# All twelve pairs of the last two tiles projected by seven products, with the order of their output products changed

## The chip, the cores and the metric

The kernel runs on one core of a Trainium2 chip. The metric is the device time of one execution in microseconds (us); the time before is the median of three runs. The trace is that of one profiled execution.

## The reference, cut to what matters

```python
scores = (q @ k^T) / sqrt(64)               # batch 8, heads 8, sequence 576, head size 64
masks  = local (0 <= i-j < 32) for heads 0-3, strided (i-j >= 0, i = j mod 32) for heads 4-7
attn   = softmax(where(mask, scores, -1e9)) @ v
x      = attn.transpose(0, 2, 1, 3).reshape(4608, 512)
a, b   = x @ w_a, x @ w_b                   # w_a, w_b: 512 x 1536
out    = (a * b) @ w_out                    # w_out: 1536 x 512
```

Inputs and output are float32; the kernel multiplies in bfloat16 and sums in float32.

## The kernel before, in words

**Tiles and slots.** The 4608 rows of x are worked off in nine tiles `t` of 512 tokens (`NT` = 9). A tile has 16 slots, and slot `16*t + s` is the unit in which everything is placed. In slots 0 to 11 the first projection is made for one block `f` of 128 of the 1536 inner columns: `a = x w_a`, `b = x w_b`, then VectorE writes `pf = a*b`. In slots 12 to 15 the output projection of the tile is made. A batch of attention has 576 tokens, so batch 7, the last, gives the last 64 tokens of tile 7 and all of tile 8. The attention steps of batch b (`S`: scores and exponential, `V`: product with v and normalisation into `xT`) are interleaved with the slots of the tiles before by a table: `LATER` by slot, `IN_Y` by the number of output products that are done. Heads are taken in eight units; `V4` to `V7` are the strided ones, whose results go straight into the fourth and third 128-row chunk of `xT` (`step_VT`: product on TensorE, a logarithm and an exponential on ScalarE, L534 and L535, two multiplications on VectorE, L541).

**Seven products.** Two places use the seven-product form of a 2x2 block product (Strassen's, in Winograd's variant).
- The output projection of tiles 2 to 8 (`FAST_Y`). Six blocks g of the inner sum, each of 128, are summed for every product k = "1" to "7" and each half q of the tokens: 14 (k, q) times 6 matmuls of 256 columns. Left operands are blocks of `pf` or sums of them, `ps`, which `fast_s(t, n, blocks)` makes on VectorE (n = 0 to 3). Sum n = 2, the operand of product 7, needs only the even half (e = 0) of each pair's `pf`. The products go to three PSUM banks X, Y, Z, and in X and Z one product is added upon another: product 6 accumulates on product 1 in X, so X must have been read out by the copy after 1 (`y_post`, ScalarE, L785) before the first matmul of 6 may write. Tiles 2 to 7 use `y_plan` (both halves q in one bank), tile 8 uses `y_tail` (one bank for each half, stored half by half).
- The first projection of some pairs g (blocks f = 2g and 2g + 1) of tiles 7 and 8 (`FAST_A`, `a_pair`): only `a` is made this way, by seven products of two matmuls of 256 columns, `b` plainly by eight matmuls of 512 columns. Its sums are `wsum_make` of w_a (in slots of tile 6) and `xsum_make(t, n)` of x.

**One pair.** `a_pair` issues on TensorE: product 1, three matmuls of b(1), product 6, one of b(1), products 7 and 2, product 5, two of b(0), products 4 and 3, two of b(0). Each product's bank is evacuated by ScalarE or added by VectorE as soon as it is there. X is read out after 1 before 6 is added. At the end `mult(1)` and then `mult(0)` form `pf` for the two blocks (L711). Its banks are given by hand: for odd g, `got[1]`, the bank of b(1), is the single buffer `tp`, and the rest are the three rotating buffers `mm`; for even g `tp` holds product 2.

**Banks.** After the start PSUM is three buffers `mm`, one `tp`, two banks `st` and two banks `o`. Plain blocks and the output projection take theirs by `mm_bank`, which counts its calls from slot 16 on and gives `tp` to every fourth:

```python
def mm_bank(shape):
    nm = "tp" if used[0] % 4 == 3 and used[0] >= 0 else "mm"
    used[0] += 1
...
        bank = {x: mm_bank([128, 2, HN]) for x in "ZXY"}     # y_plan
...
        banks = [{x: mm_bank([128, HN]) for x in "ZXY"},     # y_tail
```

A plain block takes two, a tile's output stage three (tile 1, which isn't in `FAST_Y`, four; the second halves of `y_tail` use `o`, `st` and two more). A buffer that is taken again waits until the last reader of its old content is done.

**Order.** The order on each engine is that of the program. `do(slot, ...)` and `soon` put sums behind a slot, `take` runs the attention steps.

Of the kernel before, what the change touches and what calls it, by code (L numbers as in the profile page):

```python
# [24 lines left out]
VW = 128  # L25
WCH = (0, 2, 5, 9, 12)
FAST_Y = (2, 3, 4, 5, 6, 7, 8)
FAST_A = {7: (1, 2, 3, 4), 8: (0, 1, 2, 3)}


@with_exitstack
def kernel(
# [531 lines left out]
    def step_X(b, c):  # L564
# [21 lines left out]
             10: "S6",  # L586
             11: "V5"}
    IN_Y = {2: "S7", 6: "V6", 11: "V7"}
    FN = {"Tk": step_Tk, "Tq": step_Tq, "S": step_S, "V": step_V, "X": step_X, "W": lambda b, n: fast_w(n, slice(0, 3)),
          "s": S_px, "m": S_m, "L": lead_vl, "O": rows_out, "I": rows_in, "Pk": lambda b, c: pair_up("k", c), "Pq": lambda b, c: pair_up("q", c),  # L590
          "Z": lambda b, n: zero_qz(0, nc.vector, ((1, 1),)), "D": lambda b, n: step_D(FIRST_D, 0, "k", n)}

    def run(b, slot):
# [83 lines left out]
    def a_pair(t, g):  # L677

        pf = pfs[t]
        pool, nm = ((pst, "st"), (psum4["o"], "o"))[g % 2]  # L680
        X = pool.tile([128, 2, 512], F32, tag=nm, name="ax")[:, 0, :HT]
        a = ([fsb.tile([128, TTOK], F32, tag="a_sb", name="a_sb") for _ in range(2)] if g % 2 == 0 else
             [t.rearrange("p h n -> p (h n)")[:, :2 * TTOK].bitcast(F32) for t in kT_buf[0]])
        got = {k: psum4[nm].tile([128, TTOK], F32, tag=nm, name="mm")
               for k, nm in zip((1, "Z", "Y", 0), (("mm", "mm", "tp", "mm"), ("tp", "mm", "mm", "mm"))[g % 2])}
        Z, Y = got["Z"][:, :HT], got["Y"][:, :HT]
        p7 = fsb.tile([128, HT], F32, tag="p7", name="p7")
        quarter = lambda e, k: a[e][:, HT * k:HT * (k + 1)]
        w = lambda e, j: (lambda c: wav[:, j, c, g, e])
        ws = lambda n: (lambda c: wsum_a[n][:, c, g])  # L690
        x = lambda j, k: (lambda c: x_part(t, j, k)[:, c])
        xs = lambda n: (lambda c: xsum[t][:, n, c])
        plan = {"1": (X, w(0, 0), x(0, 0)), "2": (Y, w(0, 1), x(1, 0)), "3": (X, ws(3), x(1, 1)), "4": (Z, w(1, 1), xs(3)),
                "5": (X, ws(0), xs(0)), "6": (X, ws(1), xs(1)), "7": (Z, ws(2), xs(2))}

        def P(k):
            bank, lhs, rhs = plan[k]
            for c in range(2):
                nc.tensor.matmul(bank, lhsT=lhs(c), rhs=rhs(c), start=k in "172" and c == 0, stop=c == 1, skip_group_check=True)  # L699

        x0 = TTOK * t % (XR * S)

        def b_mm(e, kks):
            f = 2 * g + e
            for kk in kks:
                nc.tensor.matmul(got[e], lhsT=wb_sb[:, kk, 128 * f:128 * (f + 1)], rhs=xT[:, kk, x0:x0 + TTOK],  # L706
                                 start=kk == 0, stop=kk == KD - 1)

        def mult(e):
            halves = lambda v_: v_.rearrange("p (a i s) -> p a i s", i=2, s=16)  # L710
            nc.vector.tensor_mul(pf[:, 2 * g + e, :].rearrange("p (i a s) -> p a i s", i=2, s=16),  # L711
                                 halves(a[e]), halves(got[e]))

        P("1")
        nc.scalar.copy(quarter(0, 0), X)
        b_mm(1, (0, 1, 2))
        P("6")
        nc.scalar.copy(quarter(1, 0), X)
        b_mm(1, (3,))
        P("7")  # L720
        nc.scalar.copy(p7, Z)
        P("2")
        nc.vector.tensor_tensor(quarter(0, 0), Y, quarter(0, 0), op=ALU.add)
        yield None
        P("5")
        nc.scalar.copy(quarter(1, 1), X)
        nc.gpsimd.tensor_tensor(quarter(1, 1), quarter(1, 1), p7, op=ALU.add)
        if (t, g - 1) in later:
            later.pop((t, g - 1))()
        b_mm(0, (0, 1))  # L730
        P("4")
        nc.vector.tensor_tensor(quarter(1, 0), Z, quarter(1, 0), op=ALU.add)
        P("3")
        nc.scalar.copy(quarter(0, 1), X)
        b_mm(0, (2, 3))
        mult(1)
        mult(0)
        yield pf[:1, 2 * g + 1, :1]

    later = {}  # L740
# [3 lines left out]
    def fast_s(t, n, gs):  # L744
        if t not in pss:
            pss[t] = nat.tile([128, FG * 5 * SW], BF16, tag="shared", name="ps").rearrange("p (n g m) -> p n g m", g=FG, n=5)
        s = pss[t][:, :, gs, :HT]
        x = pfs[t].rearrange("p (g e) (i m) -> p e i g m", e=2, i=2)[:, :, :, gs]
        a, b, op = ((x[:, 0, 1], x[:, 1, 1], ALU.add), (s[:, 0], x[:, 0, 0], ALU.subtract),
                    (x[:, 0, 0], x[:, 0, 1], ALU.subtract), (x[:, 1, 0], s[:, 1], ALU.subtract))[n]  # L750
        if (t, n) == (NT - 1, 2) and {gs.start, gs.start + 1} <= set(FAST_A[t]):
            later[t, gs.start] = lambda: nc.gpsimd.tensor_tensor(s[:, n], a, b, op=op)
            return
        nc.vector.tensor_tensor(s[:, n], a, b, op=op)
# [36 lines left out]
            nc.scalar.copy(part(0, 1), bank)  # L791

    Y_ORDER = [(x[0], int(x[1])) for x in "10 11 70 71 60 61 40 41 50 51 20 21 30 31".split()]
    TAIL_ORDER = [(x[0], int(x[1])) for x in "10 70 60 11 40 50 71 30 61 20 51 41 31 21".split()]

    def y_plan(t):

        plan, y = products(t), y_bufs()
        bank = {x: mm_bank([128, 2, HN]) for x in "ZXY"}

        def store_half(i):
            rows = out[TTOK * t:TTOK * (t + 1)].rearrange("(a i s q) c -> a s i (q c)", i=2, s=8, q=2)
            nc.sync.dma_start(out=rows[:, :, i], in_=y[i].rearrange("p q c -> p (q c)"))

        for n, (k, q) in enumerate(Y_ORDER):
            b, lhs, rhs = plan[k]
            for g in range(FG):
                nc.tensor.matmul(bank[b][:, q], lhsT=lhs(g, q), rhs=rhs(g), start=k in "172" and q == 0 and g == 0,  # L808
                                 stop=g == FG - 1, skip_group_check=True)
                if g == FG - 1:  # L810
                    if q == 1:
                        y_post(k, y, slice(0, 2), bank[b])
                        if k == "5":
                            y_post("+", y, slice(0, 2), None)
                    take(("y", t, n + 1))
                yield y
        do(16 * t + 18, store_half, 0)
        do(16 * t + 19, store_half, 1)

    def y_tail(t):  # L820
# [2 lines left out]
        banks = [{x: mm_bank([128, HN]) for x in "ZXY"},  # L823
                 {"X": psum4["o"].tile([128, 2, 512], F32, tag="o", name="end")[:, 0, :HN],
                  "Z": pst.tile([128, 2, 512], F32, tag="st", name="end")[:, 0, :HN]}]
        for k, q in TAIL_ORDER:
            b, lhs, rhs = plan[k]
            cuts = [slice(0, HN)]
            if (q, k) == (1, "2"):
                cuts = [slice(0, 128), slice(128, HN)]  # L830
            for n in cuts:
                if (q, k) == (1, "2"):
                    bank = mm_bank([128, 128])
                else:
                    bank = banks[q][b]
                for g in range(FG):
                    nc.tensor.matmul(bank, lhsT=lhs(g, q), rhs=rhs(g)[:, n], start=g == 0 and k in "172",  # L837
                                     stop=g == FG - 1, skip_group_check=True)
                    if g < FG - 1:
                        yield y  # L840
                y_post(k, y, q, bank, n)
                if k == "5":
                    y_post("+", y, q, None)
# [10 lines left out]
    def ffn_ys(t, j, mid):  # L854
        if j == 0:
            yst[t] = (y_tail if t == NT - 1 else y_plan)(t)
        for i in range(21):
            y = next(yst[t])
            if i == 10:
                mid()  # L860
        if j == 3:
            for _ in yst[t]:
                pass
        return (y[0][:1, 0, :1], None, y[1][:1, 0, HN:HN + 1], y[1][:1, 0, :1])[j]

    def ffn_y(t, j, mid):
        pf = pfs[t]
# [33 lines left out]
    with tc.manual_schedule(engines={ENG.PE, ENG.SP, ENG.Pool, ENG.DVE, ENG.Activation}):  # L901
# [76 lines left out]
        for b in range(1, B):  # L978
            for pos, names in (STEPS.get(b) or {16 * (b - 1) + x: n for x, n in LATER.items()}).items():
                steps.setdefault(pos, []).append((b, names.split()))  # L980
            if b not in STEPS:
                for n, names in IN_Y.items():
                    steps["y", b - 1, n] = [(b, names.split())]
        steps[16 * (B - 2) + 9][-1][1].append("I1")

# [4 lines left out]

        soon = {}
        for t in FAST_Y[:-1]:
            soon[16 * t + 10] = [lambda t=t: fast_s(t, 2, slice(4, 6))]
            soon[16 * t + 11] = [lambda t=t, n=n: fast_s(t, n, slice(4, 6)) for n in (0, 1)]
        do(0, fill_v, vl_buf[0])
        do(0, fill_v, vs_buf[0])
        for c in range(4):
# [21 lines left out]
                    do(g0 + g, step_D, b, z, nm, part)  # L1019
        for n in range(4):  # L1020
            do(16 * (NT - 3) + 2 * n + 2, wsum_make, n)
        do(16 * (NT - 2) - 1, xsum_make, NT - 2, 0)
        for n in (2, 1, 3):
            do(16 * (NT - 2), xsum_make, NT - 2, n)
        for n in range(4):
            do(16 * (NT - 2) + 12 + n, xsum_make, NT - 1, n)
        for h in range(HL):
            do((7, 7, 8, 9)[h], spread_vs, 1, h, nc.vector.tensor_copy)
        do(1, zero_qz, 1, nc.vector, ((1, 1),))
# [57 lines left out]
```

## Time and profile before

| | |
|---|---|
| median of 3 runs | 326.13 us (326.02 to 326.52) |
| profiled execution, its own time | 326.3 us |
| span of its trace | 324.6 us |
| granted TensorE clock, mean | 0.998 |
| TensorE (PE) busy | 317.0 us, 98% of the span |
| VectorE (DVE) busy | 258.5 us, 80% |
| ScalarE (ACT) busy | 188.9 us, 58% |
| GpSimd (POOL) busy | 160.3 us, 49% |

The profiled execution's own time is 1.7 us more than its span. In the rows, PE is TensorE's matmuls and PEld its weight loads; a row of the timeline gives the start, the duration, engine, line, operation, what is written from what, how many instructions of a kind are merged in the row, and in brackets the engine's idle time ahead of it and what ended that. A matmul's row is longer than the distance to the next one, since matmuls are pipelined; what a stage costs is read from the starts.

### The profile page before, as it was taken

Reading aid. Unit: us, or ns where it says so; the run is one execution under the profiler, and the core shown is the slowest. Engines: PE = TensorE matmul, PEld = TensorE weight load, DVE = VectorE, ACT = ScalarE, POOL = GpSimd, SP = SyncE. Lnnn points to the kernel's source line nnn. Section 1 sums busy time; section 2 is a strip of 40 time slices with the busy share of each in tenths; the row PEclk is TensorE's granted clock in tenths of the full one; section 3 lists DMA queues with packets and bytes.
Section 4 is the critical chain, followed back from the end, with each engine's and each line's share of the span. In section 5 each row is a group of like instructions: output and inputs, shape, how many; then the busy total and the mean of one; then the engine's idle time right before and its main releaser. Section 6 shows DMA issues by size and latency. Waiting matters only on the chain.

```text
span 324.6 us, 7425 instructions
## 1 busy us (share of the span) xinstructions
PE 317.0 (98%) x2651; PEld 209.4 (65%) x2680; DVE 258.5 (80%) x559; ACT 188.9 (58%) x329; POOL 160.3 (49%) x289
## 2 busy tenths in 40 slices
PE   8999999999999999999999999999999999999994
PEld 7754555455555587557999885569455966686573
DVE  6767888888778899898889888988999768837842
ACT  6763775478764576447644764476546655335441
POOL 8945837699857554853576247644013012203300
PEclk9999999999999999999999999999999999999999
DMA  9999999899999999999999979999145040004004
GB/s 154 154 204 201 203 185 174 170 181 132 139 213 136 133 95 98 118 218 131 107 107 191 172 90 108 174 174 120 43 108 140 14 129 3 0 0 131 0 3 129
DMA packets 110724, 40.43 MB, mean 125 GB/s; under 512 B 88672, under 2 KB 107744, under 8 KB 110688
## 3 DMA queue, kind: packets, MB, share of 16 engines
q0 software_dynamic: 85968, 19.48, 65.1%
q1 hardware_dynamic: 24576, 20.42, 25.3%
q8 instruction: 21, 0.34, 0.5%
q14 instruction: 15, 0.12, 0.1%
q10 hardware_dynamic: 144, 0.07, 0.1%
HBM read 39.51 MB, written 10.91 MB: 155 GB/s over the span
## 4 chain that ended last, share of the span: by engine, by line
PE 88%; DMA 6%; POOL 2%; ACT 1%; DVE 1%; issue 1%; POOLq 0%
PE mm L622 46%; PE mm L808 14%; PE mm L872 6%; PE st L388 4%; PE mm L706 4%; PE o L466 2%; PE ax L699 2%; DMA xd<-xl 2%; PE o L525 2%; DMA xT<-xd 2%; DMA vl<-in_v_dram 2%; PE mm L699 2%; PE mm L837 2%; POOL shared L197 1%; PE end L837 1%; PE ab L622 1%
## 5 line engine op out<-in xcount | busy, mean ns | idle before, releaser
L622 PE MATMUL mm<-xT,wb_sb 128*128 128x512 bf16 (+1 forms) x404 | 93.3, 354 | 0.4
L622 PE MATMUL mm<-xT,wa_sb 128*128 128x512 bf16 (+1 forms) x391 | 92.1, 353 | 1.0 <-DMA xT<-xd 0.2
L643 ACT COPY a_sb<-mm 128x512 f32<-128x512 f32 x90 | 52.7, 586 | 53.8 <-PE mm L622 51.8
L622 PEld LDWEIGHTS <-wb_sb 128*128 128x128 bf16 x416 | 40.2, 98 | 36.6 <-DVE pf L711 0.4
L1053 POOL CAST pace<-pf 1x1 f32<-1x1 bf16 x83 | 24.9, 300 | 71.2 <-DVE pf L646 51.6
L646 DVE TENSOR_TENSOR pf<-a_sb,mm 128x512 bf16<-128x512 f32 x68 | 46.2, 680 | 9.6 <-PE mm L622 8.1
L622 PEld LDWEIGHTS <-wa_sb 128*128 128x128 bf16 x416 | 37.5, 98 | 24.4 <-issue 0.5
L409 ACT ACTIVATE p<-st 72x576 bf16<-72x576 f32 (+1 forms) x56 | 36.4, 650 | 14.4 <-PE st L388 14.2
L541 DVE TENSOR_TENSOR xT<-o,xr 64x288 bf16<-64x288 f32 x48 | 21.4, 446 | 14.8 <-ACT xr L535 14.3
L808 PEld LDWEIGHTS <-ps 128*128 128x128 bf16 x288 | 28.0, 98 | 3.1
L785 ACT COPY y_sb<-mm 128x512 f32<-128x512 f32 (+1 forms) x28 | 15.6, 556 | 17.9 <-PE mm L808 15.3
L808 PE MATMUL mm<-wf,ps 128*128 128x256 bf16 x216 | 25.5, 273 | 0.0
L534 ACT ACTIVATE xr<-o 64x576 f32<-64x576 f32 x28 | 18.1, 648 | 11.9 <-PE o L525 11.6
L872 PE MATMUL mm<-wo_sb,pf 128*128 128x512 bf16 x93 | 23.0, 379 | 0.2
L243 POOL DMA_DIRECT2D vs<-in_v_dram x24 | 19.6, 820 | 4.9 <-PE mm L808 2.4
L808 PEld LDWEIGHTS <-pf 128*128 128x128 bf16 x216 | 20.3, 98 | 2.6 <-issue 0.2
L1053 POOL COPY pace<-y_sb 1x1 f32<-1x1 f32 x23 | 5.2, 226 | 33.1 <-DVE y_sb L783 19.8
L535 ACT ACTIVATE xr<-xr 64x576 f32<-64x576 f32 x28 | 19.1, 683 | 0.9
L212 POOL DMA_DIRECT2D ql<-in_q_dram x24 | 16.0, 666 | 5.8 <-DMA wo_sb<-in_moe_w_out_dram 4.9
L808 PE MATMUL mm<-wo_sb,pf 128*128 128x256 bf16 x144 | 18.5, 273 | 0.1
L212 POOL DMA_DIRECT2D kl<-in_k_dram x24 | 16.1, 670 | 4.7 <-issue 3.9
L706 PE MATMUL mm<-xT,wb_sb 128*128 128x512 bf16 x60 | 18.3, 379 | 0.1
(189 smaller groups left out, 566.6 us busy)
## 6 DMA issues: line engine op xcount, KB each, us to landing
out_dram<-y_sb SPq DMA_DIRECT2D x12, 512.0 KB, 6.0
out_dram<-y_sb SPq DMA_DIRECT2D x11, 256.0 KB, 4.0
vl<-in_v_dram POOLq DMA_DIRECT2D x6, 384.0 KB, 8.2
kl<-in_k_dram POOLq DMA_DIRECT2D x24, 72.0 KB, 3.2
ql<-in_q_dram POOLq DMA_DIRECT2D x24, 72.0 KB, 3.4
vs<-in_v_dram POOLq DMA_DIRECT2D x24, 72.0 KB, 4.3
wo_sb<-in_moe_w_out_dram POOLq DMA_DIRECT2D x4, 384.0 KB, 9.7
natk<-in_k_dram POOLq DMA_DIRECT2D x20, 72.0 KB, 3.6
```

The lines of the kernel that those rows point to most:

```text
L212: nc.gpsimd.dma_start(out=t[32 * h:32 * h + 32], in_=src[b, h].rearrange("(i y) d -> y i d", y=32))
L243: nc.gpsimd.dma_start(out=vs_buf[b % 2][:, h, :, 0:D], in_=v[b, HL + h].rearrange("(p r) d -> p r d", r=RS))
L409: nc.scalar.activation(p_flat(p)[:M, :2 * W].rearrange("p (i n) -> p i n", n=2 * n), st[:M].rearrange("p a (i n) -> p (a i) n", n=256)[:, ...
L535: nc.scalar.activation(r, r, ACT.Exp, scale=-1.0)
L541: nc.vector.tensor_mul(dst.rearrange("d (p r) -> d p r", r=RS)[:, :, G * half:G * (half + 1)], o[:64, j, :W].rearrange("d (g p) -> d p g", ...
L622: nc.tensor.matmul(ps_[:, c0:c0 + n], lhsT=w[:, kk, 128 * f:128 * (f + 1)], rhs=xT[:, kk, x0:x0 + n], start=(kk == first and c0 == 0), sto ...
L643: nc.scalar.copy(a_sb, ab[0])
L646: nc.vector.tensor_mul(pf[:, f, :].rearrange("p (i a s) -> p a i s", i=2, s=16), halves(a_sb), halves(ab[1]))
L706: nc.tensor.matmul(got[e], lhsT=wb_sb[:, kk, 128 * f:128 * (f + 1)], rhs=xT[:, kk, x0:x0 + TTOK], start=kk == 0, stop=kk == KD - 1)
L808: nc.tensor.matmul(bank[b][:, q], lhsT=lhs(g, q), rhs=rhs(g), start=k in "172" and q == 0 and g == 0, stop=g == FG - 1, skip_group_check=True)
L872: nc.tensor.matmul(ybank[j], lhsT=pf[:, f, 128 * j:128 * (j + 1)], rhs=wo_sb[:, f], start=(f == 0), stop=(f == FD - 1))
L1053: nc.gpsimd.tensor_copy(pace, done)
```

## The change

- `FAST_A` takes all six pairs of tiles 7 and 8: pairs 0 and 5 of tile 7 and pairs 4 and 5 of tile 8 go from two plain blocks each to `a_pair`.
- In pair 5 `mult(0)` comes ahead of `mult(1)`.
- The order of the output products: a lead of some products has its first five blocks done for all of them, and then their last blocks. In tile 7 the lead is 10 11 70 71, in tile 8 it is 10 70 11, where 11 is also moved ahead of 60.
- Batch 7's `V6` runs after the fifth output product of tile 6 and not the sixth, `V7` after the ninth and not the eleventh; the sums of x for tile 7 (`T0` to `T3`) follow them there, and are no longer behind slots 111 and 112.
- In tile 7 the sum n = 2 of blocks 4 and 5 follows slot 11 and not slot 10; the sums of x for tile 8 follow slots 125 and 126 and not 124 to 127; one sum of each pair of tile 8 but the last goes to GpSimd.

```diff
-FAST_A = {7: (1, 2, 3, 4), 8: (0, 1, 2, 3)}
+FAST_A = {7: range(6), 8: range(6)}
...
     IN_Y = {2: "S7", 6: "V6", 11: "V7"}
+    IN_Y_LAST = {2: "S7", 5: "V6 T0", 9: "V7 T1 T2 T3"}
...
+          "T": lambda b, n: xsum_make(NT - 2, n), ...
...
-        mult(1)
-        mult(0)
+        for e in (0, 1) if g == FG - 1 else (1, 0):
+            mult(e)
...
-        if (t, n) == (NT - 1, 2) and {gs.start, gs.start + 1} <= set(FAST_A[t]):
+        if (t, n) == (NT - 1, 2) and gs.start + 1 in FAST_A[t]:
             later[t, gs.start] = lambda: nc.gpsimd.tensor_tensor(s[:, n], a, b, op=op)
...
     Y_ORDER = [(x[0], int(x[1])) for x in "10 11 70 71 60 61 40 41 50 51 20 21 30 31".split()]
-    TAIL_ORDER = [(x[0], int(x[1])) for x in "10 70 60 11 40 50 71 30 61 20 51 41 31 21".split()]
+    TAIL_ORDER = [(x[0], int(x[1])) for x in "10 70 11 60 40 50 71 30 61 20 51 41 31 21".split()]
+
+    def blockwise(order, lead):
+
+        head = order[:lead]
+        return [(k, q, g) for k, q in head for g in range(FG - 1)] + [(k, q, FG - 1) for k, q in head] + [
+            (k, q, g) for k, q in order[lead:] for g in range(FG)]
...
-        for n, (k, q) in enumerate(Y_ORDER):
+        for k, q, g in blockwise(Y_ORDER, 4 if t in FAST_A else 0):
...
-        for k, q in TAIL_ORDER:
+        for k, q, g in blockwise(TAIL_ORDER, 3):
...
-                for n, names in IN_Y.items():
+                for n, names in (IN_Y_LAST if b == B - 1 else IN_Y).items():
...
         for t in FAST_Y[:-1]:
-            soon[16 * t + 10] = [lambda t=t: fast_s(t, 2, slice(4, 6))]
-            soon[16 * t + 11] = [lambda t=t, n=n: fast_s(t, n, slice(4, 6)) for n in (0, 1)]
+            for n in (2, 0, 1):
+                soon.setdefault(16 * t + (10 if n == 2 and t not in FAST_A else 11), []).append(
+                    lambda t=t, n=n: fast_s(t, n, slice(4, 6)))
...
-        do(16 * (NT - 2) - 1, xsum_make, NT - 2, 0)
-        for n in (2, 1, 3):
-            do(16 * (NT - 2), xsum_make, NT - 2, n)
         for n in range(4):
-            do(16 * (NT - 2) + 12 + n, xsum_make, NT - 1, n)
+            do(16 * (NT - 2) + 13 + n // 2, xsum_make, NT - 1, n)
```

More of the change, by code (lines that the diff above doesn't have):

```diff
@@ L588 @@
     IN_Y = {2: "S7", 6: "V6", 11: "V7"}
+    IN_Y_LAST = {2: "S7", 5: "V6 T0", 9: "V7 T1 T2 T3"}
     FN = {"Tk": step_Tk, "Tq": step_Tq, "S": step_S, "V": step_V, "X": step_X, "W": lambda b, n: fast_w(n, slice(0, 3)),
-          "s": S_px, "m": S_m, "L": lead_vl, "O": rows_out, "I": rows_in, "Pk": lambda b, c: pair_up("k", c), "Pq": lambda b, c: pair_up("q", c),
+          "T": lambda b, n: xsum_make(NT - 2, n), "s": S_px, "m": S_m, "L": lead_vl, "O": rows_out, "I": rows_in, "Pk": lambda b, c: pair_up("k", c), "Pq": lambda b, c: pair_up("q", c),
           "Z": lambda b, n: zero_qz(0, nc.vector, ((1, 1),)), "D": lambda b, n: step_D(FIRST_D, 0, "k", n)}
@@ L803, in store_half @@
             nc.sync.dma_start(out=rows[:, :, i], in_=y[i].rearrange("p q c -> p (q c)"))
-        for n, (k, q) in enumerate(Y_ORDER):
+        for k, q, g in blockwise(Y_ORDER, 4 if t in FAST_A else 0):
             b, lhs, rhs = plan[k]
[L807 to L816, printed above, removed]
+            nc.tensor.matmul(bank[b][:, q], lhsT=lhs(g, q), rhs=rhs(g), start=k in "172" and q == 0 and g == 0,
+                             stop=g == FG - 1, skip_group_check=True)
+            if g == FG - 1:
+                if q == 1:
+                    y_post(k, y, slice(0, 2), bank[b])
+                    if k == "5":
+                        y_post("+", y, slice(0, 2), None)
+                take(("y", t, Y_ORDER.index((k, q)) + 1))
+            yield y
         do(16 * t + 18, store_half, 0)
@@ L829, in y_tail @@
             if (q, k) == (1, "2"):
+                if g:
+                    continue
                 cuts = [slice(0, 128), slice(128, HN)]
             for n in cuts:
+                bank, gs = banks[q].get(b), (g,)
                 if (q, k) == (1, "2"):
[L833 to L836, printed above, removed]
+                    bank, gs = mm_bank([128, 128]), range(FG)
+                for g in gs:
                     nc.tensor.matmul(bank, lhsT=lhs(g, q), rhs=rhs(g)[:, n], start=g == 0 and k in "172",
@@ L840, in y_tail @@
                         yield y
+                if g < FG - 1:
+                    continue
                 y_post(k, y, q, bank, n)
@@ L863, in ffn_ys @@
                 pass
-        return (y[0][:1, 0, :1], None, y[1][:1, 0, HN:HN + 1], y[1][:1, 0, :1])[j]
+        return (None if t in FAST_A else y[0][:1, 0, :1], None, y[1][:1, 0, HN:HN + 1], y[1][:1, 0, :1])[j]
     def ffn_y(t, j, mid):
```

## The prediction

> **What bounds the kernel now.** I read the page first. The chain that ended last is TensorE's own work:
>
> ```profile
> PE 88%; DMA 6%; POOL 2%; ACT 1%; DVE 1%; issue 1%; POOLq 0%
> ```
>
> Then I cut the trace at the starts of the changed stages (columns: length, busy us and count for PE, PEld, DVE, ACT, POOL, then granted clock, DMA share, GB/s):
>
> ```profile
> 261.33:264.78 3.45, 3.40 (x17) 1.57 (x16) 2.67 (x7) 1.76 (x3) 0.24 (x1) 1.00 0.29 58
> 264.78:277.80 13.02, 12.92 (x87) 8.60 (x88) 10.13 (x22) 7.31 (x20) 3.37 (x7) 1.00 0.19 67
> 277.80:281.26 3.46, 3.46 (x17) 1.57 (x17) 3.10 (x7) 1.32 (x3) 0.64 (x3) 1.00 0.00 0
> 290.43:293.92 3.49, 3.35 (x23) 2.15 (x22) 0.96 (x3) 2.21 (x6) 0.65 (x1) 1.00 0.42 87
> 303.69:310.64 6.95, 6.90 (x33) 3.06 (x33) 5.34 (x14) 2.54 (x5) 1.19 (x4) 1.00 0.00 1
> ```
>
> These are tile 7's plain pair 0, its four seven-product pairs, its plain pair 5; tile 8's seven-product pair 0, and its two plain pairs 4 and 5. PE hardly pauses, and the output stages (281.26 to 290.43 and 310.64 to 319.84) are 9.17 and 9.20 us for 84 matmuls' worth each, 0.109 us a matmul, with no gap. So a matmul saved is time saved, and any wait put in front of PE is time lost.
>
> **What is removed.** Four plain pairs cost 3.45 + 3.46 + 6.95 = 13.86 us. The four pairs between 264.78 and 277.80 cost 13.02, 3.255 each. Four conversions give -0.84 us; that is the ceiling of the gain. The extra work on the other engines (seven evacuations a pair, GpSimd's sum) is in those 13.02 us already and hidden there.
>
> A rule speaks against this part. The Trainium skill, "TensorE: Matmul & The Clock Gate", section "Back-to-back issue gap", gives 131 ns for a sustained 512-column matmul and 81 ns for 128 columns; put between them, 256 columns would be about 98 ns (my estimate), so 14 small matmuls would cost more than the 8 large ones they replace, 1.37 against 1.05 us, and four conversions +1.3 us instead of a gain. The rows of this trace disagree with it: 512 columns follow at 0.2155 us here and 256 at 0.109, and the four pairs' 13.02 us are measured. By the rule the sum below would end at 331.3 us; it gets no chance of its own.
>
> **Tile 7, pair 0: +0.24.** A first pair behind an output stage isn't 3.255 but 3.49 us (tile 8, 290.43 to 293.92):
>
> ```profile
> 290.63 0.59 ACT L791 COPY y_sb<-mm 128x512 f32<-128x512 f32 x1 [2.03 <-PE mm L808]
> 291.11 0.38 ACT L715 COPY a_sb<-ax 128x256 f32<-128x256 f32 x1
> 291.54 0.38 PE L699 MATMUL ax<-qz1s,vl 128*128 128x256 bf16 x2
> ```
>
> The stage's last evacuation (L791) holds ScalarE, so X's copy (L715) is late, and product 6 starts at 291.54 instead of 290.43 + 0.22 + 0.65 = 291.30. Pair 0 of tile 7 will stand behind the same L791: +0.24. Its sums of x come in time (below).
>
> **Tile 6's output stage, V6 and V7 earlier: +0.52.** The steps bring their ScalarE pair ahead of a copy that X waits for. Before:
>
> ```profile
> 255.56 0.42 PE L525 MATMUL o<-p,vs 72*128 72x72 bf16 x8
> 255.81 0.59 ACT L785 COPY y_sb<-mm 128x512 f32<-128x512 f32 x1 [0.77 <-PE mm L808]
> 256.42 0.65 ACT L534 ACTIVATE xr<-o 64x576 f32<-64x576 f32 x1
> 257.10 0.68 ACT L535 ACTIVATE xr<-xr 64x576 f32<-64x576 f32 x1
> 257.14 1.47 PE L808 MATMUL mm<-wf,ps 128*128 128x256 bf16 x12
> ```
>
> Here the copy after product 6 (255.81) goes ahead of V6's two, and product 5 (257.14) finds X free. With V6 one product (6 x 0.109 = 0.66 us) earlier, at 254.90, L534 starts 0.46 later (as 259.10 to 259.56 does for V7) at 255.36, L535 ends at 256.72, and the copy, queued behind them, runs 256.74 to 257.33. Product 5 waits from 257.14 to 257.38: 0.24. V7, after product 50, starts at 258.04 (the bank `o` is free by 257.7); its pair ends at 259.86, the copy after 5 at 260.47, and product 3, due at 258.93 + 1.31 = 260.24, starts at 260.52: 0.28. T0 to T3 (0.42 each, L673) end before 262.0 on VectorE and push its last two output steps to about 263.1; the bank they free is wanted at 264.1, so they cost nothing. If the two copies squeezed in ahead, this part is 0; if ScalarE loses as much again, about 1.0. I take 0.52, the worked chain.
>
> **Tile 7's output stage: +1.13.** Two waits. How a pair ends today (pair 1 of tile 7; the next pair's first matmul is the time 0 of what follows, 268.04):
>
> ```profile
> 267.61 0.59 PE L706 MATMUL mm<-xT,wb_sb 128*128 128x512 bf16 x2
> 268.04 0.38 PE L699 MATMUL ax<-xT,wa_sb 128*128 128x256 bf16 x2
> 268.19 0.69 DVE L711 TENSOR_TENSOR pf<-kT0s,mm 128x512 bf16<-128x512 f32 x1
> 268.79 0.68 DVE L711 TENSOR_TENSOR pf<-kT0l,mm 128x512 bf16<-128x512 f32 x1
> ```
>
> mult(0), now first in pair 5, needs the last matmul (ends 268.20) plus the 0.11 that VectorE follows PE by (L646 at 281.53 after 281.42), so +0.27; mult(1) follows 0.60 later, +0.87 to +1.55. Bank Z of this stage is `tp`: `mm_bank` stood at 163 after tile 6 (28 + 5 x 27), and 163 mod 4 is 3; without the eight calls of the plain blocks this stays so. And `tp` is `got[1]` of the odd pair 5, whose last reader is mult(1). What that looks like is in the trace already, in tile 8, where plain block 8 takes `tp` behind pair 3:
>
> ```profile
> 303.84 0.69 DVE L711 TENSOR_TENSOR pf<-kT0s,mm 128x512 bf16<-128x512 f32 x1
> 304.58 0.55 PEld L622 LDWEIGHTS <-wb_sb 128*128 128x128 bf16 x4 [0.36 <-DVE pf L711]
> ```
>
> PE goes on 0.05 after mult(1) ends. So product 70, due after ten matmuls at +1.09, starts at +1.60: 0.51. Sum n = 2 of blocks 4 and 5 (0.42, to +1.90) is then in time for 70's fifth block at 2.04.
>
> The second wait is X. Before, product 60 stood 12 matmuls (1.31 us) behind the last of product 11, and the copy between needs
>
> ```profile
> 281.26 1.47 PE L808 MATMUL mm<-wo_sb,pf 128*128 128x256 bf16 x12
> 282.77 0.59 ACT L785 COPY y_sb<-mm 128x512 f32<-128x512 f32 x1 [1.59 <-PE mm L808]
> ```
>
> 0.20 after those 12 matmuls, 0.59, and 0.05 to PE: 0.84. Now the last block of 11 comes just two matmuls ahead of 60, 0.22 us. The cover is gone: 0.62.
>
> **Tile 8's output stage: +2.00.** `mm_bank` stands at 166 here (182 before, the same mod 4), so Z is `mm` and X is `tp`. The first product, 10, goes to X, so PE waits from 0 to +1.60 for mult(1), with the entire stage queued behind it. Holding back last blocks doesn't help: the bank, not the data, is late. Then 60 again: the last block of 10 is three matmuls ahead (0.33), its copy (0.20 + 0.37 for 256 columns, L785, + 0.05, and a matmul of 0.11) is needed: 0.73, wait 0.40. The rest keeps its order, and the 4.76 us from the last matmuls to the end stay.
>
> The other moves (sums for tile 8 one slot off, a sum to GpSimd, which is idle most of this stretch) lie beside PE work and cost nothing; if a sum were late it would cost its own 0.29 to 0.42 once.
>
> **Sum.** -0.84 + 0.24 + 0.52 + 1.13 + 2.00 = +3.05. The profiled execution took 326.3 us, so 329.35; the median of the runs is 0.17 lower: **329.2 us**.
>
> **Rivals.**
> - *The banks don't bind* (another count of `mm_bank`, or only the data waits). Tile 7 then waits for sum n = 2: 1.95 against 1.53, 0.42, plus 0.62; tile 8: 0.06 for its last block's sum, plus 0.40. Sum: -0.84 + 0.24 + 0.52 + 1.04 + 0.46 = +1.42, 327.5 us. Against it: the wait at 304.58 fixes the count, since block 8 got `tp` as its second bank. 0.12.
> - *Faster*: held-back last blocks cover all of pair 5's end, and the copies of X are hidden as well, so only pair 0's 0.24 is lost: -0.60, 325.5 us; without that wait 325.3. It decides for faster if the new waits together stay below 0.2 us. For it: PE stalls hardly anywhere now. Against it: 60 needs the copy of X whatever the banks. 0.04; that waits and saving cancel within 0.65 us: 0.04.
> - *More is late*: ScalarE's queue in tile 6 and VectorE's sums behind the late mults push a second wait of about 0.5 to 1 us (V7's multiplications are the last input of pair 0, b(1)'s fourth chunk). +3.8 to +4.2, about 330.3 us. For it: four consecutive VectorE steps between V7 and pair 0; against it, a slack of 1 us there. 0.12.
>
> **How the numbers follow.** The forecast has 0.68, its own range 328.5 to 329.8 (terms of tile 6 from 0 to 1.0). The range 327.5 to 330.3 takes in the first and last rivals up to their own values. A measurement of this kernel tells 0.2%, 0.65 us, from no change: faster 0.04, same 0.04, slower 0.92.
>
> **What would show it.** In the profile after: pair 0 of tile 7 about 3.5 us and the other new pairs 3.26; in tile 6's output stage two idle times of PE of a quarter of a microsecond ended by ScalarE's copies; in tile 7's one of 0.5 ended by a VectorE `pf` multiplication and one of 0.6 ended by ScalarE; at the start of tile 8's output stage one of about 1.6 us ended by the same multiplication, and then 0.4 by ScalarE. If PE flows from pair 5 into tile 8's first product without a gap, the prediction is wrong by half its size.

## The result and the profile after

The changed kernel takes 330.37 us (median of five runs, 329.31 to 330.92) against 326.52 us for the kernel before, run beside it: 1.012 times as long, 95% interval 1.010 to 1.0141. The direction was forecast; the size was not: 329.2 us was predicted, with a range that ended at 330.3.

The profiled execution of the changed kernel took 330.92 us, with a span of 329.2. The page's chain that ended last, after:

```profile
PE 84%; DMA 5%; DVE 3%; ACT 3%; POOL 2%; issue 2%; POOLq 0%; DVEq 0%; ACTq 0%
```

TensorE's share is 84% here against 88% before, and VectorE and ScalarE, which held 1% each, hold 3%. These shares alone show little: a second profile of the changed kernel (the first experiment) has 88% for TensorE again, and 2% each for the other two. What the change did is read from the changed stretches, cut at the starts of the same stages (columns as in the prediction: length, busy us and count for PE, PEld, DVE, ACT, POOL, then granted clock, DMA share, GB/s): tile 6's output stage, tile 7's six pairs, tile 7's output stage, tile 8's six pairs, and tile 8's output stage from the point where PE is free for it.

```profile
252.55:263.01 10.46, 10.27 (x110) 9.00 (x107) 7.89 (x19) 6.88 (x11) 0.27 (x2) 1.00 0.07 15
263.01:283.38 20.37, 19.69 (x135) 12.90 (x132) 15.12 (x32) 11.47 (x31) 5.03 (x10) 1.00 0.17 53
283.38:293.69 10.31, 9.51 (x86) 8.15 (x85) 6.37 (x14) 2.44 (x5) 0.34 (x2) 1.00 0.01 2
293.69:313.46 19.77, 19.69 (x134) 12.81 (x131) 15.56 (x38) 11.48 (x31) 7.68 (x15) 1.00 0.18 54
313.46:324.82 11.36, 9.68 (x91) 8.31 (x90) 4.64 (x13) 3.72 (x11) 0.88 (x3) 1.00 0.17 41
```

Cut alike, the kernel before has 9.95, 19.93, 9.17, 20.21 and 9.37 us. The differences are +0.51, +0.44, +1.14, -0.44 and +1.99: +3.64 us. What lies behind the last matmul is 0.2 us shorter (4.38 against 4.59, the differences of span and end of the last row). The rest of the two spans' difference, 1.17 us, lies ahead of tile 6's output stage (252.55 against 251.38), where the program is the same; it is taken up under the first experiment.

Where the waits are, in the timeline after. Tile 6's output stage:

```profile
256.54 0.65 ACT L534 ACTIVATE xr<-o 64x576 f32<-64x576 f32 x1 [0.33 <-PE o L525]
257.22 0.68 ACT L535 ACTIVATE xr<-xr 64x576 f32<-64x576 f32 x1
257.93 0.59 ACT L786 COPY y_sb<-mm 128x512 f32<-128x512 f32 x1
258.56 0.81 PE L814 MATMUL mm<-wf,ps 128*128 128x256 bf16 x6
```

V6's two steps now stand ahead of the copy after product 6, and product 5, due at 258.31 (twelve matmuls after 257.00), starts at 258.56. The same happens with V7 and product 3. Then pair 0 of tile 7:

```profile
262.70 0.42 DVE L674 TENSOR_TENSOR qz1l<-xT,qz1l 128x512 bf16<-128x512 bf16 x1
263.03 0.68 DVE L784 TENSOR_TENSOR y_sb<-y_sb 128x512 f32<-128x512 f32 x1
263.81 0.59 ACT L792 COPY y_sb<-mm 128x512 f32<-128x512 f32 x1 [2.16 <-DVE y_sb L784]
264.29 0.38 ACT L716 COPY a_sb<-ax 128x256 f32<-128x256 f32 x1
264.72 0.38 PE L700 MATMUL ax<-qz1l,vl 128*128 128x256 bf16 x2 [0.68 <-ACT a_sb L716]
```

The last sum of x (L674) is followed by the step "+" (L784, which adds one part of `y_sb` to another); ScalarE's copy after product 3 (L792), which overwrites a part that "+" reads, has waited for that, X's copy (L716) for L792, and product 6 for L716: it starts at 264.72 where it was due at 263.88. Tile 7's output stage:

```profile
284.24 0.68 DVE L712 TENSOR_TENSOR pf<-kT0s,mm 128x512 bf16<-128x512 f32 x1
284.98 1.27 PE L814 MATMUL mm<-wf,ps 128*128 128x256 bf16 x10 [0.34 <-DVE pf L712]
286.50 1.08 ACT L786 COPY y_sb<-mm 128x512 f32<-128x512 f32 x2 [2.93 <-PE mm L814]
287.14 1.47 PE L814 MATMUL mm<-wf,ps 128*128 128x256 bf16 x12 [0.46 <-ACT y_sb L786]
```

Product 70 goes on 0.06 after mult(1) (284.24 + 0.68), product 60 0.05 after the first copy. Tile 8's:

```profile
314.32 0.68 DVE L712 TENSOR_TENSOR pf<-kT0s,mm 128x512 bf16<-128x512 f32 x1
315.06 0.72 PE L844 MATMUL mm<-wo_sb,pf 128*128 128x256 bf16 x5 [1.44 <-DVE pf L712]
317.01 0.65 ACT L786 COPY y_sb<-mm 128x256 f32<-128x256 f32 x2 [3.36 <-PE mm L844]
317.44 0.81 PE L844 MATMUL mm<-wf,ps 128*128 128x256 bf16 x6 [0.24 <-ACT y_sb L786]
```

PE was free at 313.46 and starts at 315.06. The idle times in brackets are shorter than the losses (1.44 here against 1.60), since they are counted from a matmul's drawn-out end; the losses are taken from starts.

### The profile page after: what moved, and what is told of

It reads as the page before. It is cut to its first block, busy times and chain, and to the rows that moved or that the text cites. A ratio compares the mean times of both kernels' runs of the same rounds, so it can differ in the third digit from the quotient of the medians.

```text
span 329.2 us, 7528 instructions
## 1 busy us (share of the span) xinstructions
PE 319.0 (97%) x2704; PEld 211.7 (64%) x2704; DVE 261.8 (80%) x565; ACT 191.3 (58%) x341; POOL 162.2 (49%) x290
## 4 chain that ended last, share of the span: by engine, by line
PE 84%; DMA 5%; DVE 3%; ACT 3%; POOL 2%; issue 2%; POOLq 0%; DVEq 0%; ACTq 0%
PE mm L623 40%; PE mm L814 12%; PE mm L881 6%; PE mm L707 6%; PE st L388 4%; PE ax L700 3%; PE mm L700 2%; PE o L466 2%; PE o L525 2%; DMA xT<-xd 2%; PE mm L844 2%; DMA shared<-in_q_dram 2%; DMA xd<-xl 2%; PE end L844 1%; POOL shared L197 1%
## 5 line engine op out<-in xcount | busy, mean ns | idle before, releaser
L623 PE MATMUL mm<-xT,wa_sb 128*128 128x512 bf16 (+1 forms) x376 | 85.5, 352 | 0.9 <-DMA xT<-xd 0.9
L623 PE MATMUL mm<-xT,wb_sb 128*128 128x512 bf16 (+1 forms) x376 | 85.3, 352 | 0.0
L644 ACT COPY a_sb<-mm 128x512 f32<-128x512 f32 x82 | 48.0, 586 | 46.7 <-PE mm L623 44.6
L623 PEld LDWEIGHTS <-wb_sb 128*128 128x128 bf16 x384 | 37.1, 98 | 32.7 <-issue 0.2
L1060 POOL CAST pace<-pf 1x1 f32<-1x1 bf16 x81 | 24.1, 297 | 61.5 <-DVE pf L647 39.3
L623 PEld LDWEIGHTS <-wa_sb 128*128 128x128 bf16 x384 | 34.3, 98 | 21.4 <-issue 1.2
L647 DVE TENSOR_TENSOR pf<-a_sb,mm 128x512 bf16<-128x512 f32 x60 | 40.8, 679 | 7.4 <-PE mm L623 6.1
L707 PE MATMUL mm<-xT,wb_sb 128*128 128x512 bf16 x96 | 28.5, 379 | 0.0
L814 PE MATMUL mm<-wf,ps 128*128 128x256 bf16 x216 | 26.2, 273 | 0.9 <-ACT y_sb L786 0.5
L649 DVE TENSOR_TENSOR pf<-a_sb,mm 128x512 bf16<-128x512 f32 x22 | 14.9, 676 | 4.5 <-ACT a_sb L644 3.0
```

What stands on the lines that cost most here:

```text
L623: nc.tensor.matmul(ps_[:, c0:c0 + n], lhsT=w[:, kk, 128 * f:128 * (f + 1)], rhs=xT[:, kk, x0:x0 + n], start=(kk == first and c0 == 0), sto ...
L644: nc.scalar.copy(a_sb, ab[0])
L647: nc.vector.tensor_mul(pf[:, f, :].rearrange("p (i a s) -> p a i s", i=2, s=16), halves(a_sb), halves(ab[1]))
L1060: nc.gpsimd.tensor_copy(pace, done)
```

## Experiments

Theory 1: all of the loss is waits of PE, each with its own cause (V6 and V7 in ScalarE's queue, T1 to T3 in VectorE's, and in the output stages of tiles 7 and 8 the bank `tp` and the copy of X), and the conversions gain what was forecast. Rivals: the data of the last pair are late, not the bank; ScalarE's load is the cause, not the distance; the unchanged part became slower. Ratios are to the kernel before on the same chip, with 95% intervals.

**The changed kernel again.** No edit.

> The changed kernel once more, unaltered. Theory 1: the change costs 3.65 us between the start of tile 6's output stage and the end of the last matmul, in every execution alike (tile 6's stage 10.46 us, tile 7's pairs 20.37, its output stage 10.31, tile 8's pairs 19.77, its output stage from the last pair 11.2), and the 1.17 us by which its profile reaches tile 6's output stage later (252.55 against 251.38) is chance of the DMA traffic ahead of it: that start will come out elsewhere, between 251 and 253, with the same code. Rival: the change itself makes the unchanged part slower (another instruction stream, other times of loads): the stage starts at 252.5 again.

1.0119 (1.0102 to 1.0135), median 330.34 against 326.3 us. Tile 7's pairs and output stage:

```profile
262.54:282.92 20.38, 19.70 (x135) 12.90 (x133) 15.12 (x32) 11.48 (x31) 5.02 (x10) 1.00 0.17 53
282.92:293.22 10.30, 9.50 (x85) 8.14 (x84) 6.36 (x14) 2.44 (x5) 0.33 (x2) 1.00 0.01 2
```

The stages repeat to 0.01 us. Tile 6's output stage started at 252.08 here. Over the ten profiles of this case, whose program is the same up to there, its start lies between 250.84 (a kernel with most of the change in it) and 252.77, and both of these were taken on one chip; the kernel before has 251.38. So that part of the time scatters between executions, and the 1.17 us between the two profiles that were compared first lie within this scatter. The times of whole runs contain it too; what an edit is worth is therefore read from the stages.

**Tile 8's banks alone.**

```diff
+        used[0] += 2
         banks = [{x: mm_bank([128, HN]) for x in "ZXY"},
```

> Only the banks of tile 8's output stage: its first bank comes two places later in the count, so that X is an mm buffer (freed early in pair 5) and not tp. Theory 1 (the bank is late, not the data): the 1.44 us idle time of PE at the stage's start goes, the last blocks find pf and sums in time but for about 0.06, the 0.24 idle ahead of product 60 stays; from the end of tile 8's pairs to the last matmul 9.7 us against 11.2, the time 1.5 us shorter than the changed kernel's. Rival (the stage waits for pair 5's pf, whatever the bank): no change over 0.2 us.

1.0058 (1.0044 to 1.0071), 328.23 us. From the end of tile 8's pairs to the last matmul it is 9.75 us against 11.36, so 1.61 gone:

```profile
293.15:312.92 19.77, 19.69 (x134) 12.90 (x132) 15.55 (x38) 11.47 (x31) 7.66 (x15) 1.00 0.18 54
312.92:322.67 9.75, 9.57 (x91) 8.21 (x89) 4.64 (x13) 3.73 (x11) 0.89 (x3) 1.00 0.19 48
```
```profile
312.92 0.71 PE L845 MATMUL mm<-wo_sb,pf 128*128 128x256 bf16 x5
313.47 0.71 PE L845 MATMUL mm<-wf,ps 128*128 128x256 bf16 x5
313.78 0.68 DVE L712 TENSOR_TENSOR pf<-kT0s,mm 128x512 bf16<-128x512 f32 x1
314.01 0.71 PE L845 MATMUL end<-wo_sb,pf 128*128 128x256 bf16 x5
315.29 0.82 PE L845 MATMUL mm<-wf,ps 128*128 128x256 bf16 x6 [0.18 <-ACT y_sb L786]
```

The pair's last `pf` (mult(1), the third row) started 0.86 us after PE was free, as in the changed kernel, but the first five blocks of 10, 70 and 11 no longer waited for it. The bank was the wait; the rival falls. The wait ahead of product 60 (the last row) stays, as was expected.

**The order alone.** The lead is 10 11 in both tiles.

```diff
-        for k, q, g in blockwise(Y_ORDER, 4 if t in FAST_A else 0):
+        for k, q, g in blockwise(Y_ORDER, 2 if t in FAST_A else 0):
...
-    TAIL_ORDER = ... "10 70 11 60 40 50 71 ..."      blockwise(TAIL_ORDER, 3)
+    TAIL_ORDER = ... "10 11 70 60 40 50 71 ..."      blockwise(TAIL_ORDER, 2)
```

> Only the order of the first products: the lead is 10 11 in both tiles, so that all of 70 and 71 (tile 7) or 70 (tile 8) lie between the last block that X's copy needs and product 60. The banks stay. Theory 1: PE's idle times ahead of 60 go (0.62 and 0.40 us); in tile 7 product 70 is due at 1.31 and not 1.09 us, so its wait for tp falls from 0.51 to 0.29; in tile 8 the 1.6 us at the start stay. Tile 7's output stage 9.46 us against 10.31, in all 1.25 us shorter. Rival (ScalarE's queue is what holds 60, not the distance): the waits ahead of 60 stay above 0.3 us.

1.0069 (1.0055 to 1.0083), 328.85 us. Tile 7's output stage and tile 8's from its first matmul:

```profile
283.60:293.07 9.47, 9.34 (x85) 8.14 (x84) 6.36 (x14) 2.54 (x5) 0.33 (x2) 1.00 0.01 2
314.44:323.80 9.36, 9.36 (x90) 8.30 (x90) 3.26 (x10) 3.62 (x10) 0.17 (x1) 1.00 0.20 49
```

9.47 was expected at 9.46; the second was 9.76 in the changed kernel, so the 0.40 are gone. With 12 and 7 matmuls between the last block before X's copy and product 60, the same copy on the same ScalarE holds nobody.

**The sums T1 to T3 behind "+".**

```diff
-    IN_Y_LAST = {2: "S7", 5: "V6 T0", 9: "V7 T1 T2 T3"}
+    IN_Y_LAST = {2: "S7", 5: "V6 T0", 9: "V7", 10: "T1 T2 T3"}
```

> Only the sums T1 to T3 of tile 7: they follow output product 51 of tile 6 and not V7, so that VectorE does the step + ahead of them. Theory 1: the 0.6 us that pair 0 of tile 7 lost beyond the prediction comes from these sums: they hold the step +, which reads the buffer that ScalarE's copy after product 3 overwrites, that copy holds X's copy, and that holds product 6. Pair 0 falls from 4.1 to about 3.5 us, the rest stays. Rival (product 6 waits for T1, or for V7's rows): pair 0 stays at 4.1 us or grows, since T1 comes 0.6 us later.

1.0091 (1.0076 to 1.0105), 329.57 us. Tile 7's six pairs are 19.77 us instead of 20.37, and the timeline shows the chain dissolved:

```profile
261.31:281.08 19.77, 19.69 (x135) 12.91 (x132) 15.10 (x33) 11.46 (x31) 5.01 (x10) 1.00 0.18 54
```
```profile
260.31 0.69 DVE L784 TENSOR_TENSOR y_sb<-y_sb 128x512 f32<-128x512 f32 x1
261.50 0.58 ACT L792 COPY y_sb<-mm 128x512 f32<-128x512 f32 x1 [1.56 <-PE mm L814]
261.99 0.38 ACT L716 COPY a_sb<-ax 128x256 f32<-128x256 f32 x1
262.42 0.38 PE L700 MATMUL ax<-qz1l,vl 128*128 128x256 bf16 x2
```

"+" comes ahead of the sums, the copy L792 now waits for PE and not for "+", and product 6 starts 1.11 us after the pair's first matmul, not 1.71. T1 came later and nobody minded. These 0.60 us are shown to come from the place of three sums in VectorE's queue.

**V6 and V7 earlier, alone, on the kernel before.**

```diff
-                for n, names in IN_Y.items():
+                for n, names in ({2: "S7", 5: "V6", 9: "V7"} if b == B - 1 else IN_Y).items():
```

> The kernel before with one part of the change alone: V6 after output product 60 and V7 after 50 of tile 6; nothing else. Theory 1: each pair of ScalarE steps goes ahead of a copy that X waits for, so tile 6's output stage is 10.46 us and not 9.95, with idle times of PE of about 0.25 us ahead of products 50 and 30, and the kernel 0.5 us slower than before. Rival (that stage is longer in the changed kernel because of the sums T0 to T3 there): 9.95 us here.

1.0023 (1.0007 to 1.0039), 327.57 against 326.8 us.

```profile
251.41:261.87 10.46, 10.27 (x110) 8.99 (x107) 7.56 (x17) 6.88 (x11) 0.45 (x3) 1.00 0.07 15
261.87:281.80 19.93, 19.93 (x123) 11.73 (x121) 14.98 (x32) 10.37 (x25) 4.24 (x10) 1.00 0.18 54
```

The stage is 10.46 us with no sum in it; the 0.51 belong to V6 and V7 alone, and tile 7's pairs, with a plain pair 0, keep their 19.93.

**Tile 7's banks alone.**

```diff
         plan, y = products(t), y_bufs()
+        used[0] += t in FAST_A
         bank = {x: mm_bank([128, 2, HN]) for x in "ZXY"}
```

> The changed kernel with tile 7's output banks alone moved: Z is an mm buffer and not tp (and, by the count, tile 8's stage has Z in tp and X in mm). Theory 1: in tile 7 PE then waits for the next thing, the sum n = 2 of blocks 4 and 5, so the stage is 10.2 us against 10.31, and ScalarE's copy ahead of 60 stays at about 0.6. In tile 8 product 10 starts at once, 70, due at 0.55 us, waits for mult(1) until 1.60, and 60 waits 0.4 as before: the stage's start loses 1.05 and not 1.60, so the kernel is 0.65 us shorter than the changed one. Rival (the first use of tp is no wait of its own): tile 7's stage 9.8 us or less.

1.007 (1.0056 to 1.0084), 329.29 us.

```profile
282.32:292.53 10.21, 9.51 (x86) 8.14 (x85) 6.38 (x14) 2.44 (x5) 0.34 (x2) 1.00 0.01 2
```
```profile
284.26 0.83 PE L815 MATMUL mm<-wf,ps 128*128 128x256 bf16 x6 [0.24 <-DVE ps L755]
```

With the bank free, product 70 starts, and its fifth block waits for the sum n = 2 (L755): 10.21 us, as expected. Here the bank and the data are late together, and freeing one is worth 0.1 us. In tile 8 the count's other effect came out too: from the end of the pairs to the last matmul 10.89 us, 1.47 more than in the version below, where 1.05 + 0.40 were expected. The two stages are 0.57 us shorter together than in the changed kernel, and 0.65 was expected. The ratios differ by more, 0.0049 or 1.6 us; the rest lies outside these stages and was not traced (this profile reached tile 6's output stage at 251.49, the two of the changed kernel at 252.55 and 252.08).

**A version without the waits.** Pair 0 of tile 7 plain, V6, V7 and tile 7's sums as before, and:

```diff
-FAST_A = {7: range(6), 8: range(6)}
+FAST_A = {7: range(1, 6), 8: range(6)}
...
             mult(e)
+            if g == FG - 1 and e == 0:
+                fast_s(t, 2, slice(5 if t == NT - 1 else 4, 6))      # taken out of its later place
...
+        used[0] += t in FAST_A        # y_plan:  Z, X, Y all mm
+        used[0] += 1                  # y_tail:  the same
...                                    # leads 10 11, order 10 11 70 60 40 50 71 ..., as above
```

> A version without the waits: pair 0 of tile 7 plain, V6, V7 and the sums of tile 7 where they were before; the other eleven pairs by seven products; the output banks of tiles 7 and 8 off tp; lead 10 11 in both, in tile 8 the order 10 11 70 60; the sum n = 2 of the last blocks between mult(0) and mult(1). Theory 1: three conversions at 0.2 us stay and nothing is lost: tile 6's output stage 9.95, tile 7's pairs 19.7, output stages 9.2 each, no idle time of PE over 0.1 us from pair 5 into the products; 0.6 us shorter than before, about 325.7 (0.2% faster). Rival (the end of the last pair can't be covered): 0.3 us or more stay at the start of each output stage, and the time is that of before or longer.

0.9974 (0.9959 to 0.9989), 326.08 against 326.8 us: faster than both kernels. The five stages:

```profile
251.93:261.88 9.95, 9.95 (x110) 8.99 (x107) 6.63 (x15) 6.88 (x11) 0.78 (x3) 1.00 0.06 12
261.88:281.61 19.73, 19.73 (x129) 12.34 (x126) 15.61 (x34) 10.88 (x28) 4.54 (x10) 1.00 0.18 54
281.61:290.78 9.17, 9.17 (x86) 8.21 (x84) 6.55 (x14) 2.54 (x5) 0.33 (x2) 1.00 0.01 2
290.78:310.55 19.77, 19.69 (x134) 12.90 (x132) 15.55 (x38) 11.47 (x31) 7.67 (x15) 1.00 0.17 53
310.55:319.97 9.42, 9.42 (x91) 8.21 (x89) 4.82 (x13) 3.83 (x11) 1.00 (x3) 1.00 0.21 52
```

Both output stages are back at their old length, to 0.05 us, with the last pair by seven products in front; PE's busy time fills the length in all but the first-pair wait of tile 8. The stages sum to 0.59 us less than before (68.04 against 68.63), as three conversions at about 0.2 should. Most of its moves were run alone above; the sum n = 2 ahead of mult(1) was not.

**One matmul more ahead of product 6 in tile 8's pair 0.** On the version above, all four matmuls of b(1) stand ahead of product 6.

```diff
-        b_mm(1, (0, 1, 2))
+        b_mm(1, (0, 1, 2, 3) if g == 0 else (0, 1, 2))
         P("6")
...
-        b_mm(1, (3,))
+        if g:
+            b_mm(1, (3,))
```

> The version without the waits, and in pair 0 of tile 8 all four matmuls of b(1) stand ahead of product 6, so that X's copy has one more matmul (0.2155 us) to be done. Theory 1: pair 0 of tile 8 falls from 3.49 to about 3.28 us; 0.2 us less than the version without it, 0.8 less than before. Rival (product 7's bank or ScalarE's queue takes the wait's place): pair 0 stays at 3.45 us or more.

0.9973 (0.9958 to 0.9988): no difference to be told from the version above. Pair 0 is 3.47 us instead of 3.49.

```profile
291.25 0.38 PE L700 MATMUL ax<-qz1s,vl 128*128 128x256 bf16 x2
291.66 0.37 ACT L719 COPY a_sb<-ax 128x256 f32<-128x256 f32 x1 [0.47 <-PE ax L700]
292.08 0.38 PE L700 MATMUL ax<-qz1s,vl 128*128 128x256 bf16 x2
```

Product 6 starts 1.12 us after the pair's first matmul, almost where it was, because one matmul more now stands in front of it; its own copy (L719) then has only products 7 and 2 to hide behind, and product 5, due at 291.90, waits until 292.08. The wait moved; the rival holds.

## Why the prediction was right in its mechanisms and wrong in its size

Point by point, in the forecast's order, forecast and measured (us):

| step | forecast | measured |
|---|---|---|
| conversions, two in tile 8 (with the 0.03 wait ahead of block 8) | -0.44 | -0.44 |
| tile 7: two conversions and the first-pair wait | -0.40 + 0.24 | +0.44 |
| V6 and V7 earlier | +0.52 | +0.51 |
| tile 7's output stage | +1.13 | +1.14 |
| tile 8's output stage | +2.00 | +1.99 |
| sum | +3.05 | +3.64 |

- **The step that failed** is the sentence of the tile 6 part that T0 to T3 "push its last two output steps to about 263.1; the bank they free is wanted at 264.1, so they cost nothing". It followed only the PSUM bank that the last step frees. It missed that "+" reads the part of `y_sb` that ScalarE's copy after product 3 overwrites: delayed by T1 to T3, "+" held that copy, behind which X's copy of pair 0 stood in ScalarE's queue. The first-pair term, sized 0.24 from tile 8's pair 0, where nothing stands ahead of "+", was 0.84. Moving the three sums behind "+" brought it back (20.37 to 19.77 us).
- **The banks** did what the count of `mm_bank` said: mult(1) was forecast to end 1.55 after PE was free, and PE to go on at 1.60; it was 1.60 in tile 8. The rival that the banks don't bind is refuted there by the run that moved them. In tile 7 the sum n = 2 was nearly as late as the bank, and moving the bank alone gave 0.10 us.
- **The rival "more is late"** had the place (VectorE's steps between V7 and pair 0) and nearly the price, but the wrong carrier: it named V7's multiplications as pair 0's last input, while pair 0 waited for ScalarE.
- **The faster rival** needed the waits to stay below 0.2 us; they came to 4.5 (0.51, 0.84, 1.14 and 1.99).
- **The rule of the Trainium skill** ("TensorE: Matmul & The Clock Gate", section "Back-to-back issue gap": 131 ns for a sustained 512-column matmul) would have made the conversions a loss, by the prediction's estimate from it. The trace disagrees: tile 8's pairs fell by 0.44 us.
- The same page of the Trainium skill says in its Part 3, "The mechanism", that matmuls start strictly in order. The run that moved tile 8's banks agrees: in the changed kernel the whole stage stood behind product 10 until 315.06, though 70 and 11 write other banks; with the bank of 10 moved, 10, 70 and 11 started 0.00, 0.55 and 1.09 us after PE was free.

Of the measured +3.85 us, 3.64 - 0.2 = 3.4 are read off the stages and the end. The remaining 0.4 is inside the ratio's interval (3.3 to 4.6 us) and of the size of the scatter ahead of tile 6's output stage; whether a part of it belongs to the change was not settled. Nor was it found why the end behind the last matmul is 0.2 us shorter with the new order. The forecast also started from 326.13, the median before, and the kernel before took 326.52 beside the change: 0.39 us of the distance from 329.2 to 330.37 come from there, 0.59 from the stages, nearly all of it the step that failed.

## What to carry to other kernels

Where TensorE is full, as here, saved matmuls are worth their distances (three conversions: 0.59 us of a forecast 0.64), and every reordering has to be tried against three questions, not one: is the data there, is the bank free (who is its last reader, by the real rotation count), and has the copy between two accumulations its cover. When work is put into another engine's queue, follow not only what that work frees but every instruction that now stands behind it, and what those hold in turn, buffers in SBUF included; here three sums of 0.4 us reached TensorE over two engines. And a gain that is fenced in by waits may be had by moving the waits: three of the four conversions that came with a loss of 1.2% gain 0.26% (0.11 to 0.41) with other banks and another order.

## What the runs showed of the hardware that was not expected

From tile 6's output stage on, stages whose program is the same repeat to 0.01 us between executions, at a DMA share of 0.01 to 0.18. The start of that stage scatters over 1.9 us (250.84 to 252.77) with the same program; the stretch ahead of it is the one with heavy loads (mostly 0.9 and more in the page's DMA row), but that these are the cause was not shown. PE's 1.6 us pause at the head of tile 8's output stage left the granted clock at 1.00.
